# Four more one-element-per-64-KB reads on the ScalarE DMA ring, ahead of the vector c

## The chip, the cores and the metric

The kernel runs on one core of a Trainium2 chip. The metric is the device time of one execution in microseconds (us). Before the change it was 245.06 us, the median of 4 runs.

## The reference

One transformer block on x of 2048 rows by 512 columns, in bf16, with its modulation computed from a vector c:

```python
mod = (silu(c) @ w_mod).reshape(1, 6, 1, 512)       # w_mod 512 x 3072
sa, ca, ga, sb, cb, gb = mod[:, 0], ..., mod[:, 5]
h = layernorm(x) * (1 + ca) + sa
x = x + ga * A(h, wqkv, wo)                          # 32 heads of 16, window of 8 keys, 2 apart
h = layernorm(x) * (1 + cb) + sb
x = x + gb * ((gelu(h @ w_gate) * (h @ w_up)) @ w_down)   # 512 -> 1792 -> 512
```

In A each query attends to the keys at its own row and 2, 4, ... 14 rows before it. The weights are wqkv (512 x 1536), wo (512 x 512), w_gate and w_up (512 x 1792) and w_down (1792 x 512).

## The kernel before, in words

The 2048 rows are cut into five groups of 256, 256, 512, 512 and 512 rows. For each group the kernel normalizes the rows, transposes them, projects to q, k and v, attends, projects back, normalizes again, and runs the gated feed-forward part; the groups overlap. TensorE does the projections and the sums over head dimensions, VectorE the elementwise products of the attention, ScalarE most copies out of PSUM and the activations.

All work is recorded first, as operations with an engine each, and then emitted in one fixed sequence, the list ORDER. Nothing is decided at run time: each engine executes its instructions in that order. The change does not alter the list.

DMAs are issued on two rings: SP's for all loads, stores and transposes, and ScalarE's for four small ones at the very start. In the built program the completion of DMAs is counted on eight semaphores, called lanes here, that are handed out in turn over both rings. A DMA that takes a lane first waits on its issuing engine until the DMA that had the lane before it has landed. So each DMA waits for the one that stands eight places ahead in the program.

The start of the kernel before, by engine:

- ScalarE issues three touches (lines 390 to 398) and then the load of c into `crow` (line 396). A touch reads one pair of bf16 values (4 bytes) from each 64 KB of a tensor into a scratch tile, `touched`, that nothing reads: 48 pairs of w_mod, 24 of wqkv, 32 of x. After that ScalarE loads its activation table and computes scT = silu(c) (line 451).
- SP loads x rows 0 to 255, 256 to 511 and 512 to 1023, then two 512-column blocks of w_mod (line 402), the first two thirds of wqkv (line 384), x rows 1024 to 1535, the last third of wqkv, x rows 1536 to 2047, half of wo, another block of w_mod and the first half of w_gate. The rest of w_gate, w_up and w_down follow between 47 and 72 us.
- TensorE runs 14 warm-up matmuls on zeros (line 435), turns c into columns (`c_ps`, line 448, needs `crow`), runs nine fillers on zeros (line 440), computes the modulation columns `modT_ps` from scT and the two w_mod blocks (line 462), transposes the normalized rows `tp` (line 550) between them, and starts the first projection (`qkv_ps`, line 607).

The first half of w_up is issued at 60.2 us and the second at 62.9 (line 384), into the tile `Wu`; the feed-forward matmuls `g_ps` and `u_ps` (line 800) read `Wg` and `Wu`.

Of the kernel before, what the change touches and what calls it, by code (L numbers as in the profile page):

```python
# [12 lines left out]
BF16 = mybir.dt.bfloat16  # L13
# [52 lines left out]
def _ap(base, free_dims, offset=0):  # L66
    return bass.AP(base.tensor, base.offset + offset, [list(base.ap[0])] + [list(d) for d in free_dims])
# [147 lines left out]
def kernel(  # L215
# [13 lines left out]
    nc = tc.nc  # L229
    P = 128  # L230
# [13 lines left out]
    pl = Plan(tc)  # L244
# [14 lines left out]
    def ctile(shape, dtype, name):  # L259
        t = Tl(None, shape, dtype, name)  # L260
        t.t = const.tile(shape, dtype, name=name)
        return t
# [108 lines left out]
    def load_x(lo, hi, p, after=()):  # L371
        return dma(131e3 * (hi - lo), lambda dq: dq.dma_start(
            out=xs[lo // 4][:, lo % 4:lo % 4 + hi - lo, :],
            in_=A_x[0, lo * P:hi * P, :].rearrange("(c p) d -> p c d", p=P)),
            w=[(xs[lo // 4], c % 4) for c in range(lo, hi)], pri=p, after=after,
            bw=340e3)
# [8 lines left out]
            out=t[:], in_=src[:, lo:hi].rearrange("(t p) n -> p t n", p=P)), w=[t], pri=p, bw=bw, late=late, after=after)  # L385


    touched = ctile([P, 4, 2], BF16, "touched")

    def touch(i, src, n, p):  # L390
        page = 32768
        dma(1.0, lambda dq: dq.dma_start(out=touched[0:n, i, :], in_=bass.AP(src.tensor, src.offset, [[page, n], [1, 2]])),
            w=[(touched, i)], pri=p, ring="act")
# [2 lines left out]
    act(0.5, lambda: nc.scalar.dma_start(out=crow[:], in_=c), w=[crow], pri=-1003, lat=1.7, after=pl.ops[-1:])  # L396
    touch(1, A_wqkv, 24, -1002)
    touch(2, A_x, 32, -1001)
    touches = pl.ops[-2:]
    load_x(0, 2, -1000)  # L400
    for b in (1, 0):
        dma(524e3, lambda dq, b=b: dq.dma_start(
            out=wm01[:, :, b * D:(b + 1) * D], in_=w_mod[:, b * D:(b + 1) * D].rearrange("(t p) n -> p t n", p=P)),
# [7 lines left out]
    for d4 in range(4):  # L411
        dma(131e3, lambda dq, d4=d4: dq.dma_start(
            out=woP[32 * d4:32 * d4 + 32, :, :],
            in_=bass.AP(A_wo.tensor, A_wo.offset + 4 * D * d4, [[16 * D, H], [D, 4], [1, D]])), w=[(woP, d4)],
# [8 lines left out]
    for i in range(2):  # L423
        lo, hi = i * FT // 2, (i + 1) * FT // 2
        dma(918e3, lambda dq, lo=lo, hi=hi: dq.dma_start(
            out=WdP[:, lo:hi, :], in_=B_w_down[lo * P:hi * P, :].rearrange("(t p) n -> p t n", p=P)),
# [422 lines left out]
    for g in range(NG):  # L849
# [11 lines left out]
        if g == PLAIN:  # L861
            for f0 in range(0, FT, 2):
                dve(0.6, lambda f0=f0: nc.vector.tensor_tensor(
                    out=WdP[:, f0:f0 + 2, :], in0=WdP[:, f0:f0 + 2, :], in1=_ap(gbB[:], [[0, 2], [1, D]]),
# [34 lines left out]
```

## Time and profile before

| | |
|---|---|
| time, median of 4 runs | 245.06 us (244.79 to 246.78) |
| the profiled execution | 245.41 us, span 243.7 us |
| TensorE matmul busy | 234.6 us, 96% of the span |
| VectorE, ScalarE, GpSimd busy | 163.4, 148.4, 25.8 us |
| DMA | 29.10 MB, mean 119 GB/s |
| first touch, issue to landing | 2.2 us |
| x touch, issue to landing | 3.1 us |

The profile is of one execution; the span runs from its first to its last instruction. Times in the lines shown below are microseconds from the start of the span; in the lines of instructions in order of time the first number is the start, the second the duration, then engine, source line, operation, and in brackets the idle time before it with what ended it. ACTq and SPq are DMA issues of ScalarE and SP. PEld is TensorE's weight load. A line of the DMA queues gives packets, MB, and the time of the packets as a share of 16 engines over the window.

### The profile page before, as it was taken

How to read it: one execution, taken by the hardware profiler on the slowest of the kernel's cores; microseconds unless marked ns; L12 is line 12 of the kernel's file. 1: busy time of each engine (PE TensorE's matmuls, PEld its weight loads, DVE VectorE, ACT ScalarE, POOL GpSimd, SP SyncE). 2: the span in 40 equal slices, each digit the busy share in tenths (PEclk: the TensorE clock that was granted, in tenths of full speed). 3: DMA queues.
4: the chain of work that ended last, by engine and by line, in shares of the span. 5: the costliest groups of instructions: out<-in, count | busy, mean ns of one | idle time of the engine just before them, and what ended most of it. 6: DMA issues, size and time to landing. Idle time of an engine off the chain costs nothing.

```text
span 243.7 us, 4304 instructions
## 1 busy us (share of the span) xinstructions
PE 234.6 (96%) x1660; PEld 128.0 (53%) x1680; DVE 163.4 (67%) x317; ACT 148.4 (61%) x278; POOL 25.8 (11%) x45
## 2 busy tenths in 40 slices
PE   7799999999999999999999999999999999999993
PEld 3499555544469645675444444444444444444461
DVE  4878998999999999669985577983422413221222
ACT  2188798678958663894588866327467442665400
POOL 1287212002000300120000011000000100000000
PEclk9999999999999999999999999999999999999999
DMA  5998999898999438268021904210000412000011
GB/s 173 351 316 263 191 194 236 186 232 199 260 279 251 141 90 176 65 175 151 7 65 51 219 16 89 43 43 1 3 0 0 106 27 86 0 0 0 3 43 43
DMA packets 38970, 29.10 MB, mean 119 GB/s; under 512 B 14117, under 2 KB 38054, under 8 KB 38950
## 3 DMA queue, kind: packets, MB, share of 16 engines
q1 hardware_dynamic: 38800, 28.83, 49.9%
q8 instruction: 13, 0.21, 0.4%
q14 instruction: 7, 0.06, 0.1%
q10 hardware_dynamic: 150, 0.00, 0.0%
HBM read 21.40 MB, written 4.28 MB: 105 GB/s over the span
## 4 chain that ended last, share of the span: by engine, by line
PE 68%; DVE 16%; DMA 8%; issue 2%; POOL 2%; ACT 2%; SPq 0%; DVEq 0%; ACTq 0%; POOLq 0%
PE y_ps L827 20%; PE u_ps L800 20%; PE g_ps L800 18%; PE x_ps L777 4%; DMA Wu<-in_B_w_up_dram 4%; DMA wqkv<-in_A_wqkv_dram 3%; DVE pq L660 3%; DVE pq L654 3%; DVE pv L752 3%; PE o_ps L762 2%; POOL rstd L522 2%; DVE st L516 2%; DVE xn L526 1%; DMA x_sg<-in_A_x_dram 1%; PE LT L670 1%
## 5 line engine op out<-in xcount | busy, mean ns | idle before, releaser
L800 PE MATMUL u_ps<-h2T,Wu 128*128 128x512 bf16 (+1 forms) x280 | 54.4, 336 | 0.8 <-DMA Wu<-in_B_w_up_dram 0.4
L800 PE MATMUL g_ps<-h2T,Wg 128*128 128x512 bf16 (+1 forms) x280 | 54.7, 337 | 0.1
L827 PE MATMUL y_ps<-WdP,hht 128*128 128x512 bf16 (+1 forms) x230 | 49.1, 366 | 0.4
L809 ACT ACTIVATE gl<-g_ps 128x512 bf16<-128x512 f32 x56 | 33.0, 603 | 25.4 <-PE g_ps L800 25.2
L603 PE MATMUL qkv_ps<-hT,wqkv 128*128 128x512 bf16 (+1 forms) x229 | 43.7, 339 | 0.1
L812 DVE TENSOR_TENSOR hht<-gl,ub 128x512 bf16<-128x512 bf16 x56 | 22.6, 422 | 29.2 <-ACT ub L811 20.9
L811 ACT CAST ub<-u_ps 128x512 bf16<-128x512 f32 x56 | 31.7, 589 | 15.4 <-PE u_ps L800 12.2
L800 PEld LDWEIGHTS <-Wu 128*128 128x128 bf16 x280 | 27.0, 98 | 23.1 <-issue 1.5
L800 PEld LDWEIGHTS <-Wg 128*128 128x128 bf16 x280 | 27.0, 98 | 23.0 <-issue 1.5
L827 PEld LDWEIGHTS <-hht 128*128 128x128 bf16 x238 | 23.1, 98 | 24.6 <-issue 0.4
L522 POOL TENSOR_TENSOR rstd<-rstd,neghalf 128x2 f32<-128x2 f32 x16 | 17.5, 1094 | 162.7 <-DVE rstd L511 140.5
L603 PEld LDWEIGHTS <-wqkv 128*128 128x128 bf16 x232 | 24.9, 114 | 13.6 <-issue 1.3
L654 DVE TENSOR_TENSOR pq<-qT,kT 128x2048 bf16<-128x2048 bf16 x24 | 28.8, 1213 | 0.3
L746 DVE TENSOR_TENSOR pv<-e,vR 128x2048 bf16<-128x2048 bf16 x24 | 28.4, 1216 | 0.0
L538 ACT ACTIVATE h2T<-h2T,modT,scl 128x512 bf16<-128x512 bf16 (+1 forms) x20 | 13.2, 726 | 14.8 <-DMA h2T<-xn 14.8
L840 DVE TENSOR_TENSOR ot<-y_ps,x_sg 128x512 bf16<-128x512 f32 (+1 forms) x13 | 8.2, 647 | 18.5 <-PE y_ps L827 18.5
L781 DVE SCALAR_TENSOR_TENSOR x_sg<-x_ps,x_sg 128x512 bf16<-128x512 f32 x16 | 11.0, 687 | 14.2 <-PE x_ps L777 7.2
L777 PE MATMUL x_ps<-woP,oT 128*128 128x512 bf16 x57 | 14.9, 379 | 0.7 <-DVE rinv L723 0.4
L508 ACT ACTIVATE xn<-x_sg,xsum 128x512 bf16<-128x512 bf16 x16 | 11.5, 721 | 4.3 <-DVE xsum L505 4.3
L516 DVE BATCH_NORM_STATS2 st<-x_sg 128x6 f32<-128x512 bf16 x16 | 10.6, 679 | 3.2 <-DMA x_sg<-in_A_x_dram 3.2
L619 ACT CAST kT<-qkv_ps 128x512 bf16<-128x512 f32 x16 | 9.4, 596 | 1.8 <-PE qkv_ps L603 1.8
L619 ACT CAST qT<-qkv_ps 128x512 bf16<-128x512 f32 x16 | 9.4, 597 | 1.3 <-PE qkv_ps L603 1.3
(93 smaller groups left out, 200.0 us busy)
## 6 DMA issues: line engine op xcount, KB each, us to landing
vR<-scr SPq DMA_DIRECT2D x24, 260.0 KB, 5.3
wm<-in_w_mod_dram SPq DMA_DIRECT2D x6, 512.0 KB, 6.7
vR<-scr SPq DMA_DIRECT2D x8, 264.0 KB, 5.2
out_dram<-ot SPq DMA_DIRECT2D x15, 128.0 KB, 1.8
Wg<-in_B_w_gate_dram SPq DMA_DIRECT2D x2, 896.0 KB, 10.9
Wu<-in_B_w_up_dram SPq DMA_DIRECT2D x2, 896.0 KB, 5.8
WdP<-in_B_w_down_dram SPq DMA_DIRECT2D x2, 896.0 KB, 13.9
scr<-vT SPq DMA_DIRECT2D x6, 264.0 KB, 2.8
```

The costliest lines, as they stand in the source:

```text
L516: dve(0.59, lambda i=i, st=st, c0=c0: nc.vector.bn_stats(out=st[:, i, :], in_=x[g, c0 + i]), r=[x.key(g, c0 + i)], w=[(st, i)], pri=p)
L522: gp(0.65, lambda rstd=rstd: nc.gpsimd.tensor_tensor(out=rstd[:], in0=rstd[:], in1=neghalf[:, 0:2], op=ALU.pow), r=[rstd, neghalf], w=[rst ...
L603: nc.tensor.matmul(ps[:, j - j0, :], lhsT=wqkv[b][:, dt, j:D:4], rhs=h_cols(hT, g, dt), start=(dt == 0), stop=(dt == DT - 1))
L619: act(0.475, lambda t=t, off=off, j0=j0, ps=ps: nc.scalar.copy(out=t[:, j0:j0 + nj, off:off + n], in_=ps[:]), r=[ps], w=[(t, j) for j in r ...
L654: dve(1.14, lambda j=j, wg=wg, t=pq[m]: nc.vector.tensor_tensor(out=t[:], in0=_ap(q[g][:, j, 0:n], [[0, 4], [1, n]]), in1=_ap(k[g][:, j, : ...
L746: dve(1.14, lambda jj=jj, jl=jl, wg=wg, t=pv[m]: nc.vector.tensor_tensor(out=t[:], in0=_ap(e[:, wg, :], [[0, 4], [1, n]]), in1=vR[g][jj][: ...
L777: nc.tensor.matmul(x1_ps[:], lhsT=oT[:, j, c4 * P:(c4 + 1) * P], rhs=woP[:, j, :], start=(j == 0), stop=(j == 3))
L800: nc.tensor.matmul(ps[:, ft - f0, :], lhsT=Wt[ft // 7][:, dt, ft % 7 * P:(ft % 7 + 1) * P], rhs=h_cols(h2, g, dt), start=(dt == 0), stop=( ...
L809: act(0.485, lambda gl=gl, ps=gu[0]: nc.scalar.activation(out=gl[:], in_=ps[:], func=ACT.Gelu_apprx_tanh), r=[gu[0]], w=[gl], pri=p, table ...
L811: act(0.475, lambda ub=ub, ps=gu[1]: nc.scalar.copy(out=ub[:], in_=ps[:]), r=[gu[1]], w=[ub], pri=p)
L812: dve(0.335, lambda gl=gl, ub=ub, ht=ht: nc.vector.tensor_tensor(out=ht[:], in0=gl[:], in1=ub[:], op=ALU.mult), r=[gl, ub], w=[ht], pri=p)
L827: nc.tensor.matmul(y_ps[:], lhsT=hh[ft // nf][:, ft % nf, c4 * P:(c4 + 1) * P], rhs=WdP[:, ft, c0:c0 + w], start=(ft == 0), stop=(ft == FT ...
```

## The change

Four more touches follow the x touch on ScalarE's ring, ahead of `crow`: 8 pairs of wo, 28 each of w_gate, w_up and w_down, into a scratch tile that grows from 4 to 8 columns. They are put into the function of the x touch's operation, so ORDER and the operations in it stay as they are.

```diff
-    touched = ctile([P, 4, 2], BF16, "touched")
+    touched = ctile([P, 8, 2], BF16, "touched")
...
     touch(1, A_wqkv, 24, -1002)
     touch(2, A_x, 32, -1001)
+    first = pl.ops[-1].fn
+
+    def more():
+        first()
+        for i, (src, n) in enumerate(((A_wo, 8), (B_w_gate, 28), (B_w_up, 28), (B_w_down, 28))):
+            nc.scalar.dma_start(out=touched[0:n, 3 + i, :], in_=bass.AP(src.tensor, src.offset, [[32768, n], [1, 2]]))
+
+    pl.ops[-1].fn = more
     touches = pl.ops[-2:]
```

## The prediction

> **What bounds the kernel now.** I read the page first, then the chain of waits over the first 20 us, then the instructions of that stretch in order of time, then the DMA queues in small windows, and last the one later place where a touched tensor is waited for. The page says that TensorE is the bound as a whole:
>
> ```profile
> span 243.7 us, 4304 instructions
> PE 234.6 (96%) x1660; PEld 128.0 (53%) x1680; DVE 163.4 (67%) x317; ACT 148.4 (61%) x278; POOL 25.8 (11%) x45
> ```
>
> So what delays the first real matmul delays the end, unless an idle place later takes it up, and there are only 9.1 us of TensorE idle time in the whole span. The change works on the start. The chain there:
>
> ```profile
> 0.81 2.96 DMA x_sg<-in_A_x_dram
> ...
> 3.79 8.26 DMA wqkv<-in_A_wqkv_dram
> ...
> 12.10 0.84 PE qkv_ps L607 x6
> ```
>
> The first projection waits for the first wqkv third, which lands at 12.05. From 7 us on the DMA engines are full (375, 380, 362, 348, 349 GB/s in the five microseconds from 7 to 12), so the landings of the two w_mod blocks and of wqkv are set by bytes. TensorE is nearly as late, and this is what the chain hides:
>
> ```profile
> 1.26 4.49 PE L435 MATMUL warm_ps<-warm 128*128 128x512 bf16 x14 [1.26 <-DVE neghalf L306]
> 5.71 0.25 PE L448 MATMUL c_ps<-one,crow 1*128 1x1 bf16 x4
> 5.88 2.12 PE L440 MATMUL warm_ps<-warm 128*128 128x512 bf16 x9
> 9.09 0.55 PE L462 MATMUL modT_ps<-scT,wm 128*128 128x1 bf16 x16 [1.08 <-DMA wm<-in_w_mod_dram]
> 9.50 0.61 PE L550 MATMUL tp<-ident,xn 128*128 128x128 bf16 x8
> ...
> 12.10 0.84 PE L607 MATMUL qkv_ps<-hT,wqkv 128*128 128x256 bf16 x6
> ```
>
> The reader is to see an in-order queue: `crow` (the vector c) must be there before `c_ps`, nine filler matmuls stand behind it, and only then come the modulation columns. The one spare is the 1.08 us before 9.09. From 9.09 to 12.10 TensorE has about 0.1 us to spare. The ScalarE queue that brings `crow`:
>
> ```profile
> 0.81 0.44 ACTq L392 DMA_DIRECT2D touched<-in_w_mod_dram  x1
> 1.28 0.64 ACTq L392 DMA_DIRECT2D touched<-in_A_wqkv_dram  x1
> 1.95 0.33 ACTq L392 DMA_DIRECT2D touched<-in_A_x_dram  x1
> 2.31 0.30 ACTq L396 DMA_DIRECT2D crow<-in_c_dram  x1
> ```
>
> It is issued by 2.61, but TensorE gets it at 5.71. Why so late is seen in the DMA queues by window (q1 is SP's ring, q10 ScalarE's). These lines are of 2.93 to 3.80 us, of 3.80 to 4.80 and of 5.20 to 5.31:
>
> ```profile
> q1 hardware_dynamic: 321, 0.31, 100.2%
> q10 hardware_dynamic: 40, 0.00, 2.6%
> ...
> q10 hardware_dynamic: 42, 0.00, 2.2%
> ...
> q10 hardware_dynamic: 1, 0.00, 0.5%
> ```
>
> The 64 packets of the first touch come from 1.88 to 2.68. The second touch's 36 packets start only at 2.93, in threes, and by the packet records each three starts 6 ns after an engine has ended its share of the first x transfer. The third touch's follow in the same way from 3.84, behind the second x transfer. `crow`'s single 1 KB packet comes at 5.21, in the middle of the third x transfer. So each ScalarE DMA waits on each engine for a portion of SP's stream.
>
> **What the Trainium skill says.** "DMA: Bandwidth & Descriptors", section "Queues, rings and completion order", says that a DMA engine takes the rings in turn and drains a whole packet (some 9 to 17 descriptors) of one before it goes to the next. The trace agrees: an x transfer of 256 KB is 16 one-KB pieces per engine, and one such portion lies between two touches. The same page, "Why a DMA increments its semaphore by 16 and not by 1", says that a DMA over few partitions uses the lowest-numbered engines; then engine 0 serves every touch and `crow` as well, so on that engine they stand in one line. No run here shows the engine numbers. "TensorE: Matmul & The Clock Gate", Part 1, puts the clock back to half after an idle window of about 3.4 us; the trace shows the other half of this: 14 warm-up matmuls in 4.49 us are about seven at 0.427 and seven at 0.216, and the nine fillers at 0.235 each are at full speed. On what a first read of a 64 KB stretch costs, no page bears.
>
> **The change, part by part.** Instruction order is unchanged on TensorE, VectorE and GpSimd. On ScalarE four DMAs stand between the x touch and `crow`. Since all DMAs take the eight lane semaphores in turn, four more in front shift who waits for whom. In the built program the touches of w_up and w_down wait for the w_mod touch and for x rows 0 to 255, `crow` waits for x rows 256 to 511; on SP the w_mod blocks wait for the wqkv touch and the x touch (before: nothing and the w_mod touch), the first wqkv third for the wo touch, x rows 1024 on for the w_gate touch, and two more for the w_up and w_down touches. From the third w_mod block on each waits for the same transfer as before.
>
> *ScalarE's issue.* wo and w_gate touches are issued by 3.0 (two of about 0.33). The w_up touch needs 3.0, when the w_mod touch landed (0.81 + 2.2). The w_down touch needs 3.77, when the first x landed. `crow` needs the second x: 3.1 us to landing from an issue at about 1.3, so 4.4. It goes out at 4.45 to 4.75 instead of 2.31. That alone would cost little, for even now it is not served before 5.21.
>
> *The ring.* At 5.21, where `crow` stood, engine 0 serves the wo touch. Then four turns follow: w_gate, w_up, w_down, `crow`, each behind a portion of SP's stream. One 1 KB packet is 16 x 0.87 x 1.002 / 321 = 43 ns, so 16 are 0.7 us; the measured step between touches (2.93 to 3.84) is 0.9. I take 0.8, for part of the portions run at the stalled rates of 4 to 7 us (217 to 282 GB/s): 4 x 0.8 = 3.2 us. `c_ps` starts at 5.71 + 3.2 = 8.9. Bounds: no turn paid, if SP's ring is empty when they come or one turn takes several DMAs, gives `crow` at 4.75 + 0.6 = 5.4, so +0.2; five turns at 0.9 give +4.5.
>
> *TensorE.* `c_ps` and the fillers end 2.3 us after 8.9, at 11.2; the modulation columns start there and not at 9.09: 3.2 - 1.08 = +2.1 us. The rest, 3.0 us of packed work, ends in the first projection at 14.2. scT (0.2 us on ScalarE) lies beside the fillers, and so does the table load of 1.28 us, which starts at about 4.8.
>
> *SP.* The first w_mod block goes at about 4.1 instead of 2.34, the second at about 5.1 (the x touch lands at 1.95 + 3.1), the first wqkv third at about 6. The 1 MB of x occupies the engines until 5.4 to 7.4, so the stream should hardly gap; at worst it loses 1 us, and w_mod and wqkv are then at 10.1, 11.6 and 13.1, still ahead of a TensorE that is at 11.2, 12.7 and 14.2. Cost nothing, covered by the late `crow`; without that cover up to 1 us. The 142 or so extra packets of 9 ns over 14 engines cost 0.1 us each: nothing.
>
> *What the touches may bring.* wo is needed at 46.6 us and has long landed. w_gate's first load runs at 359 GB/s (19.5 to 22 us) untouched, w_down's at 332 to 348 (77 to 81); there is nothing to gain. Only w_up's first load starts slowly, 161 GB/s until 62.6 and then 380, and its second part is waited for:
>
> ```profile
> PEld L800 <- DMA Wu<-in_B_w_up_dram: 0.9, 1, 0.9
> PE u_ps L800 <- DMA Wu<-in_B_w_up_dram: 0.4, 1, 0.4
> ```
>
> The slow stretch holds 1016 packets under 512 B of a transpose, so it is explained without a first read. Gain 0 to 0.4 us, at most 0.9; I take 0.
>
> *Sum.* +2.1 us on the profiled execution, 245.41 to 247.5. That execution stands 0.35 above the median, so the median goes from 245.06 to about 247.1. I take up nothing later: the stretch from 16 to 60 us is data-driven through VectorE (about 95% busy from 25 to 60), so it shifts as a whole.
>
> **The rivals.** *The cover holds* (not slower): `crow` is served in the gaps that SP's later issues leave on its ring, and comes less than 1.1 us later. For it: the new waits do thin SP's stream around 5 us; DMA share in 4 to 5 us is only 0.81 already. Against it: x of 512 rows is still queued then. It decides where `c_ps` starts before 6.8. Time 245.1. With the w_up gain of up to 0.9 on top, *a small gain*: 244.4.
>
> *The clock falls back or the line is longer.* TensorE is idle from 5.75 to 8.9, 3.1 us; at some 0.3 us more a whole idle window is possible and nine fillers take 9 x 0.427 = 3.8 us instead of 2.1: +3.8 and more, 249. Five turns without a fallback give 4.5 - 1.1 = +3.4, 248.5. For it: the stalled rates between 4 and 7 us. Against it: idleness must cover a window whole.
>
> *DMA starved:* the late w_mod issues leave the engines empty for 2 us or more and the wqkv third lands at 14 or later. The size would be that of my forecast, by another path; the chain would then show DMA, not `crow`.
>
> **How the numbers follow.** Forecast (+1.1 to +2.9 us, by `crow` or by starved DMA) 0.47; cover holds 0.27; small gain 0.06; clock or longer line 0.20. A measurement of this kernel can tell about 1%, 2.45 us, from no change. Slower by more than that: 0.20 and a quarter of the forecast's chance, 0.32. Faster by more than that: 0.03, only from causes that I don't see. The rest, 0.65, is within it. Range: 244.4 (the gain's end) to 249.2 (+3.8 and a little).
>
> **What would show it.** `c_ps` at about 8.9 instead of 5.71, the first projection at 14.2 instead of 12.10 with an idle TensorE before `c_ps` of some 3 us, released by `crow`; w_mod waits at 9.09 gone; the nine fillers in about 2.1 us; a first load of w_up with the same slow start at 60 us plus the shift. I am wrong if `c_ps` starts before 6.8, if the shift of the first projection is not found at the end of the span, or if the wait for w_up at 71.3 is gone and the time with it.

## The result, and the profile after

The kernel after takes 245.78 us (median of 42 runs, 244.65 to 247.87), beside 245.06 us for the kernel before, run on the same chip. The ratio is 1.003, with a 95% interval of 1.0017 to 1.0044: a loss of 0.7 us, between 0.4 and 1.1. It is slower, by about a third of the 2.1 us that was forecast. The profiled execution of after took 247.78 us and is one of 6 in 42 (247.35 to 247.87) in which TensorE's mean granted clock was under 0.995 of full, here because the clock was at half from 8.9 to 12.3 us; the others have a median of 245.68, and the first experiment below shows the same kernel at full clock.

The page of after:

```profile
span 246.1 us, 4308 instructions
PE 236.5 (96%) x1660; PEld 128.6 (52%) x1680; DVE 163.4 (66%) x317; ACT 148.3 (60%) x278; POOL 25.6 (10%) x45
```

TensorE's instructions of the start in order of time (start, busy time, what, and in brackets the idle time before it with its releaser):

```profile
1.25 5.27 PE L443 MATMUL warm_ps<-warm 128*128 128x512 bf16 x14 [1.25 <-DVE neghalf L306]
8.49 0.25 PE L456 MATMUL c_ps<-one,crow 1*128 1x1 bf16 x4 [1.97 <-DVE xn L534]
8.68 3.80 PE L448 MATMUL warm_ps<-warm 128*128 128x512 bf16 x9
12.30 0.55 PE L470 MATMUL modT_ps<-scT,wm 128*128 128x1 bf16 x16
...
14.87 0.82 PE L615 MATMUL qkv_ps<-hT,wqkv 128*128 128x256 bf16 x6
```

`c_ps` starts at 8.49 (5.71 before) and the first projection at 14.87 (12.10 before). The bracket at 8.49 names VectorE, but the weight load of `c_ps`, which reads `crow`, waited longer and for the DMA:

```profile
PEld L456 <- DMA crow<-in_c_dram: 2.5, 1, 2.5
```

The nine fillers take 3.80 us here, at half clock, against 2.12 before. The DMA issues on ScalarE in order of time, and then those on SP:

```profile
2.30 0.34 ACTq L404 DMA_DIRECT2D touched<-in_A_wo_dram  x1
...
3.19 0.32 ACTq L404 DMA_DIRECT2D touched<-in_B_w_up_dram  x1
3.89 0.40 ACTq L404 DMA_DIRECT2D touched<-in_B_w_down_dram  x1
4.58 0.23 ACTq L396 DMA_DIRECT2D crow<-in_c_dram  x1
```
```profile
3.94 1.54 SPq L410 DMA_DIRECT2D wm<-in_w_mod_dram  x2
5.65 1.64 SPq L384 DMA_DIRECT2D wqkv<-in_A_wqkv_dram  x2
```

Each issue stands where the prediction had worked it out from the lanes: `crow` at 4.58 (4.45 forecast), w_mod at 3.94 (4.1), wqkv at 5.65 (6). The prediction went wrong in what it derived from them.

### The profile page after: what moved, and what is told of

Read it like the earlier page. It is cut to its first block, busy times and chain, and to the rows that moved or that the text cites. A ratio compares the mean times of both kernels' runs of the same rounds, so it can differ in the third digit from the quotient of the medians.

```text
span 246.1 us, 4308 instructions
## 1 busy us (share of the span) xinstructions
PE 236.5 (96%) x1660; PEld 128.6 (52%) x1680; DVE 163.4 (66%) x317; ACT 148.3 (60%) x278; POOL 25.6 (10%) x45
## 4 chain that ended last, share of the span: by engine, by line
PE 72%; DVE 19%; issue 2%; POOL 2%; ACT 2%; DMA 1%; DVEq 0%; ACTq 0%; POOLq 0%
PE y_ps L835 20%; PE u_ps L808 19%; PE g_ps L808 19%; PE x_ps L785 4%; DVE pq L662 4%; DVE pq L668 3%; DVE st L524 3%; DVE pv L760 3%; PE o_ps L770 2%; POOL rstd L530 2%; PE warm_ps L448 2%; PE LT L678 2%; DVE xn L534 2%; PE qkv_ps L611 1%; DMA x_sg<-in_A_x_dram 1%
## 5 line engine op out<-in xcount | busy, mean ns | idle before, releaser
L546 ACT ACTIVATE h2T<-h2T,modT,scl 128x512 bf16<-128x512 bf16 (+1 forms) x20 | 13.2, 727 | 14.5 <-DMA h2T<-xn 14.5
```

## The experiments

Each was timed beside the kernel before; the ratio is to that, with its 95% interval, and need not be the plain quotient of two medians. `c_ps` and "first projection" are the starts of these matmuls (the first `qkv_ps`) in one profiled execution, 5.71 and 12.10 in the kernel before. "Full clock" below means executions with a mean granted TensorE clock of 0.995 or more.

| kernel | median us | ratio | c_ps | first projection |
|---|---|---|---|---|
| after again | 246.05 | 1.0038 (1.0015 to 1.006) | 7.56 | 12.87 |
| fillers ahead | 245.83 | 1.0027 (1.0009 to 1.0045) | 8.66 | 12.84 |
| three fillers | 245.89 | 1.003 (1.0009 to 1.005) | 7.46 | 14.22 |
| load of c first | 245.91 | 1.0036 (1.0015 to 1.0056) | 7.24 | 12.14 |
| c waits, no reads | 247.2 | 1.005 (1.0023 to 1.0077) | 8.39 | 13.08 |
| two reads | 245.55 | 1.0006 (0.9977 to 1.0035) | 7.29 | 12.93 |
| tiny reads | 245.66 | 1.0033 (1.0017 to 1.0048) | 8.05 | 13.00 |
| reads by GpSimd | 245.5 | 1.0003 (0.998 to 1.0027) | 6.00 | 13.36 |
| no reads at all | 245.27 | 1.0016 (0.9997 to 1.0036) | 5.87 | 12.09 |
| late reads | 245.5 | 1.0014 (0.9992 to 1.0035) | 6.81 | 12.21 |
| pages of w_mod | 246.01 | 1.0029 (1.0007 to 1.0051) | 7.80 | 12.62 |

### After again

No edit.

> The changed kernel once more, for a profile of its usual execution. The one profiled had the nine fillers at half clock (3.80 us for 2.12), and its 247.78 us was among the slowest of its runs. Theory (crow late, fillers behind it): c_ps again at about 8.5, fillers in about 2.1 us where the clock stays at full, first projection at 12.30 - 1.7 + 2.6 = 13.2 us (12.10 before, 14.87 in the profile after), time 245.8. Rival (the DMA stream is what is late): first projection waits for wqkv, and the time does not depend on the fillers' clock.

The loss is there again, and stands at full clock too (median 245.98 of 12, beside 245.09). TensorE's start:

```profile
7.56 0.25 PE L456 MATMUL c_ps<-one,crow 1*128 1x1 bf16 x4 [0.97 <-DMA crow<-in_c_dram]
7.74 2.12 PE L448 MATMUL warm_ps<-warm 128*128 128x512 bf16 x9
9.75 0.55 PE L470 MATMUL modT_ps<-scT,wm 128*128 128x1 bf16 x16
...
11.36 0.55 PE L470 MATMUL modT_ps<-scT,wm 128*128 128x1 bf16 x16
...
12.87 0.84 PE L615 MATMUL qkv_ps<-hT,wqkv 128*128 128x256 bf16 x6
```

`c_ps` starts 1.85 us later than in the kernel before, the first modulation columns 0.66, the projection 0.77. So c came earlier than expected (8.5), and so did the projection (13.2). The chain that ended last (start, duration, what) says what set it:

```profile
2.31 3.73 DMA touched<-in_A_wo_dram
...
6.06 6.77 DMA wqkv<-in_A_wqkv_dram
...
12.87 0.84 PE qkv_ps L615 x6
```

SP issues the first wqkv third when the read of wo, whose lane it takes, has landed at 6.04. The third lands at 12.83 (12.05 before), and the projection starts at once. That is the mark of the rival. The second set of columns waits for the stream as well. Here are the waits of TensorE's weight loads in the first 16 us (total, times, longest), and then the start by stretches of 1 us, where the last three numbers are the granted clock, the DMA share and GB/s:

```profile
PEld L470 <- DMA wm<-in_w_mod_dram: 1.0, 2, 0.6
```
```profile
7.00:8.00 1.00, 0.44 (x6) 0.30 (x7) 1.00 (x5) 0.15 (x1) 0.14 (x2) 1.00 0.66 202
8.00:9.00 1.00, 1.00 (x6) 0.46 (x5) 1.00 (x5) 0.02 (x1) 0.79 (x1) 1.00 0.79 241
9.00:10.00 1.00, 1.00 (x14) 0.45 (x13) 1.00 (x3) 0.00 (x0) 0.00 (x0) 1.00 0.95 303
10.00:11.00 1.00, 1.00 (x23) 0.71 (x19) 0.84 (x3) 0.17 (x1) 0.00 (x0) 1.00 0.97 324
11.00:12.00 1.00, 0.85 (x19) 0.53 (x19) 0.00 (x0) 0.06 (x1) 0.00 (x0) 1.00 1.08 380
```

The kernel before moved 375, 380, 362, 348 and 349 GB/s in these five microseconds, so 1814 KB; here it is 1450 KB, less 364. From 4 to 7 us it was 46 KB more, which leaves 318 KB, or 0.9 us at 350 GB/s. SP's loads were issued later, behind lanes, and the DMA engines ran partly empty at 7 to 9 us. So there are two late paths side by side, c and the stream. Here the stream sets the projection. By c alone it would have started at about 12.3; this is an estimate from the columns at 9.75 and the 2.55 us that the work from there takes where no DMA is waited for ("c waits" below). The next kernels take one path or the other away.

### Fillers ahead

In `emit`, where `ccol` is the operation of `c_ps`:

```diff
+        i = pes.index(self.ccol)
+        pes[i].fill, pes[i + 1].fill = pes[i].fill + pes[i + 1].fill, 0
...
+    pl.ccol = pl.ops[-1]
```

> The kernel after, with the nine filler matmuls put ahead of c_ps, behind the 14 warm-up matmuls, so that nothing but scT stands between the late load of c and the modulation columns, and TensorE is not idle before c_ps. Theory one (the late c with its nine fillers is what delays the first projection): the modulation columns start at about 9.1 and the first projection at about 12.1 to 12.4; median 245.1 to 245.3, as the kernel before. Theory two (in the usual execution the stream of w_mod and wqkv, issued later because of the new lane waits on SP, is as late as c): the columns and the projection wait for DMA, first projection at about 12.7 to 12.9; median 245.7 to 246.0. Both expect the executions with fillers at half clock to be gone, since TensorE no longer idles before c_ps.

TensorE in order of time:

```profile
8.66 0.25 PE L458 MATMUL c_ps<-one,crow 1*128 1x1 bf16 x4
9.16 0.54 PE L473 MATMUL modT_ps<-scT,wm 128*128 128x1 bf16 x16 [0.26 <-ACT scT L462]
...
11.39 0.55 PE L473 MATMUL modT_ps<-scT,wm 128*128 128x1 bf16 x16 [0.79 <-DMA wm<-in_w_mod_dram]
...
12.84 0.84 PE L618 MATMUL qkv_ps<-hT,wqkv 128*128 128x256 bf16 x6
```

Theory two: with c's path shortened, the first columns start at 9.16, nearly as early as before, and the time turns up again one step later as a wait of 0.79 us for w_mod. The projection is 0.74 us late, nearly all of it by the stream, and the loss stays (1.0027). That no execution would fall below full clock was a miss: the mean granted clock was under 0.995 in 6 of 22.

### Three fillers

```diff
+            q.fill = min(q.fill, 3)
```

> The kernel after, with three filler matmuls instead of nine behind c_ps: 6 x 0.235 = 1.4 us less TensorE work behind the late c. Theory one (late c and fillers bind): the modulation columns start 1.1 to 1.4 us earlier than in the kernel after, first projection at about 12.1; median 245.1. Theory two (the stream of w_mod and wqkv binds as well): columns wait for DMA w_mod at about 9.7, first projection at 12.7 to 12.9; median 245.7 to 246.0. If the thinner fillers let the clock fall back to half, modT and the transposes run at twice their time and it is 247 or more under either.

Theory two again by the time, 1.003. The 1.3 us taken out of the fillers became a wait for the stream, as TensorE's order of time shows:

```profile
7.64 0.82 PE L449 MATMUL warm_ps<-warm 128*128 128x512 bf16 x3
9.98 0.59 PE L471 MATMUL modT_ps<-scT,wm 128*128 128x1 bf16 x16 [1.52 <-DMA wm<-in_w_mod_dram]
```

In this execution TensorE fell to half clock at about 9.7, ahead of these columns, which is why its first projection is as late as 14.22. Of all 22 executions 7 had a mean clock under 0.995; the other 15 have a median of 245.52, still 0.5 above the kernel before at full clock (245.00).

### Load of c first

The four reads are issued behind the load of c, not ahead of it:

```diff
+    crow_op = pl.ops[-1]
...
-    first = pl.ops[-1].fn
+    first = crow_op.fn
...
-    pl.ops[-1].fn = more
+    crow_op.fn = more
```

> The same four touches, but issued after the load of c on ScalarE; SP's lane waits stay as in the changed kernel. Theory: c_ps back at about 5.7, so the cost goes, time 245.1 to 245.5 (what is left is SP's stream, whose wqkv third lands some 0.6 us later). Rival (the stream, or the touches themselves, cost the time): 245.8 as in the changed kernel. If touching the later weights brings anything, it shows here: below 244.7.

c is issued at 2.31 and SP's loads wait as in the kernel after. The theory's `c_ps` at 5.7 was missed: it starts at 7.24, behind warm-up matmuls that ended late. The ratio keeps the loss (1.0036), so some loss doesn't need c's late issue. How much is less sure: 7 of the 22 executions were below full clock, and the other 15 have a median of 245.44, 0.35 above that of the kernel before (245.09). The profiled execution doesn't show the loss at the start. Its projection is at 12.14, with the w_mod and wqkv bytes served only 0.2 us later than before (the first 2.62 MB at 10.86 us against 10.62, by the packet records); its first `u_ps` comes 0.24 us later, mostly by a longer wait for w_up (0.57 against 0.37), and that is most of the 0.3 by which its span is longer.

### c waits, no reads

The kernel before, with a ScalarE copy of one x column ahead of the load of c, so that c is issued late and SP's loads are as before:

```diff
+    def load_c():
+        nc.scalar.copy(out=touched[:, 3, 0:1], in_=xs[0][:, 0, 0:1])
+        nc.scalar.dma_start(out=crow[:], in_=c)
...
+    act(0.5, load_c, w=[crow], pri=-1003, lat=1.7, after=pl.ops[-1:])
```

> The kernel before, with no added DMA; ScalarE copies one column of x rows 0 to 127 into scratch before it issues the load of c, so the load waits for the first x transfer (3.8 us) and goes out at about 4.1 instead of 2.31; a second activation-table load comes with the copy. Two theories of why c arrives at 8.49 after the change. Late issue (the load needs about 3 us from its issue whatever stands in the ring): c_ps at about 7.5. Ring turns (as predicted: each touch ahead of it costs a turn of 0.8): nothing stands ahead, so c_ps at 5.7 to 6.3. Time: 245.1 to 245.6 under the first, 245.1 under the second.

ScalarE's issue of the load of c, and TensorE's first use of it, with the columns and the projection that follow:

```profile
3.84 0.26 ACTq L398 DMA_DIRECT2D crow<-in_c_dram  x1
```
```profile
8.39 0.25 PE L452 MATMUL c_ps<-one,crow 1*128 1x1 bf16 x4 [2.25 <-DMA crow<-in_c_dram]
...
10.53 0.54 PE L466 MATMUL modT_ps<-scT,wm 128*128 128x1 bf16 x16
...
13.08 0.82 PE L611 MATMUL qkv_ps<-hT,wqkv 128*128 128x256 bf16 x6
```

A late c alone costs too, if it is late enough: `c_ps` at 8.39 gives a projection at 13.08, and a ratio of 1.005. The stream is whole here (382 and 380 GB/s at 7 to 9 us) and no weight load between the columns and the projection waits for a DMA, so the 2.55 us from 10.53 to 13.08 are the packed length of that stretch. The median of 247.2 lies further off than the ratio: 6 of the 16 executions were below full clock, and the other 10 have a median of 246.22. The profiled one also happens to wait 1.77 us for w_up. This is also the run that breaks the forecast's ring step. No added read stands ahead of `crow`, the ring's last other packet went at 4.44 us, and still `crow`'s packet comes at 7.83, 4.0 us after its issue.

### Two reads

Only w_up and w_down of the four.

```diff
-        for i, (src, n) in enumerate(((A_wo, 8), (B_w_gate, 28), (B_w_up, 28), (B_w_down, 28))):
+        for i, (src, n) in enumerate(((B_w_up, 28), (B_w_down, 28))):
```

> The kernel after with only the reads of w_up and w_down. The load of c then waits for the first w_mod read (landed at about 3.0) and is issued at about 3.1 instead of 4.5; SP's two w_mod blocks still wait for the wqkv and x reads as in the kernel after. Theory one (c's late issue is the larger part): c_ps at about 6.4 to 6.8, fillers done before 9.0, loss 0 to 0.3 us; median 245.0 to 245.4. Theory two (the late stream on SP is enough by itself): c_ps as early, but the modulation columns wait for w_mod at 9.4 to 9.8 and the projection for wqkv, first projection at 12.5 to 12.9; median 245.5 to 245.9.

TensorE in order of time:

```profile
7.29 0.25 PE L456 MATMUL c_ps<-one,crow 1*128 1x1 bf16 x4 [1.39 <-DMA crow<-in_c_dram]
...
11.42 0.55 PE L470 MATMUL modT_ps<-scT,wm 128*128 128x1 bf16 x16 [0.42 <-DMA wm<-in_w_mod_dram]
```

c was issued at 3.21 as expected, but `c_ps` started at 7.29, not at 6.4 to 6.8. The profiled projection (12.93) is theory two's to within 0.03, and so is the median of 245.55; but the interval of the ratio holds 1 and also the loss of the kernel after, so by time this run decides nothing.

### Tiny reads

The same four DMAs, with one pair each:

```diff
-        for i, (src, n) in enumerate(((A_wo, 8), (B_w_gate, 28), (B_w_up, 28), (B_w_down, 28))):
+        for i, (src, n) in enumerate(((A_wo, 1), (B_w_gate, 1), (B_w_up, 1), (B_w_down, 1))):
```

> The kernel after with each of the four added reads cut to one element: the same four DMAs at the same places, so c and SP's loads wait for the same lanes, but 4 packets on the ScalarE ring instead of the 142 added, and 88 stretches of 64 KB fewer are read ahead. Theory one (the lane waits are the loss): c issued at 4.4 to 4.6, SP's w_mod blocks at 3.9 and 5.1 to 5.6, less than 300 GB/s moved in 7 to 9 us, first projection at 12.7 to 12.9; median 245.7 to 246.1. Rival (the packets of the reads, in between SP's, are the loss): SP's stream keeps about 350 GB/s from 7 us on, first projection at 12.1 to 12.4; median 245.0 to 245.4.

ScalarE's issue of the load of c; TensorE in order of time; the stretches of 7 to 9 us:

```profile
4.57 0.23 ACTq L396 DMA_DIRECT2D crow<-in_c_dram  x1
```
```profile
8.05 0.25 PE L456 MATMUL c_ps<-one,crow 1*128 1x1 bf16 x4 [0.77 <-DVE xn L534]
...
13.00 0.84 PE L615 MATMUL qkv_ps<-hT,wqkv 128*128 128x256 bf16 x6
```
```profile
7.00:8.00 1.00, 0.28 (x1) 0.00 (x0) 1.00 (x5) 0.00 (x0) 0.19 (x2) 1.00 0.95 255
8.00:9.00 1.00, 0.95 (x8) 0.57 (x9) 1.00 (x5) 0.17 (x1) 0.79 (x1) 1.00 0.92 270
```

This is the decisive one. ScalarE's ring carried 158 packets, 8 more than before, where the kernel after has 292; and everything is as in the kernel after: c's issue, the 2.9 us from it to its packet (3.3 in after), the thin stream at 7 to 9 us, the wqkv third (it lands at 12.95), and the time, 1.0033 (1.0017 to 1.0048). The first projection, at 13.00, is 0.1 beyond theory one's window. The loss is in the four DMAs' places in the lane order, not in what they read.

### Reads by GpSimd

The four reads with `nc.gpsimd.dma_start`, behind its first masks, so that no lane of the other two rings moves:

```diff
-            nc.scalar.dma_start(out=touched[0:n, 3 + i, :], in_=...)
+            nc.gpsimd.dma_start(out=touched[0:n, 3 + i, :], in_=...)
```

> The same four reads at the same time, but issued by GpSimd in its idle time between 1.6 and 5.8 us, so that the loads on the ScalarE and SP rings wait for exactly the lanes that they wait for in the kernel before. Theory one (the change loses by the lane waits, of c and of SP's loads, not by the reads): c issued at 2.3, w_mod and wqkv as in the kernel before, first projection at 12.1 to 12.2; median 244.9 to 245.3. Rival (the 142 extra packets or the rings' turns cost the stream or c the time): first projection at 12.6 or later, median 245.6 to 246.0. If GpSimd's issuing takes over 1.05 us for each, its rstd at 5.79 is late, and so the first normalised rows: up to 1 us more, with VectorE and not DMA named in front of the transposes.

Issued at 1.5 to 3.8 us, with rstd at 5.82 (5.79 before), so GpSimd lost nothing. The ratio is 1.0003: the reads without the lane waits can't be told from no change. The median of 245.5 lies between the two theories' windows, but the kernel before had 245.2 beside it in this comparison, and only the ratio counts. The profiled execution misses theory one's 12.1, though: the first columns wait for w_mod until 9.77, and then TensorE runs at half clock from about 11.4 to 14.8 us, which makes most of its 13.36. Why w_mod was 0.7 us late there is open.

### No reads at all

The kernel before with its own three reads left out as well.

```diff
+    for o in (pl.ops[-4], pl.ops[-2], pl.ops[-1]):
+        o.fn = lambda: None
```

> The kernel before without its three small reads: the load of c is first on the ScalarE ring, and the first eight loads wait for no lane. Theory one (a first read of a 64 KB stretch costs nothing that can be seen): w_mod and wqkv land as in the kernel before or a few tenths earlier, first projection at 11.8 to 12.1; median 244.8 to 245.2. Rival (the small reads do prepare the large loads): w_mod and wqkv are served at less than 340 GB/s, first projection at 12.6 or later; median 245.6 or more.

Theory one by the profile: the columns at 9.07, the projection at 12.09, and the stream of the kernel before to within a few GB/s, here by stretches of 1 us:

```profile
7.00:8.00 1.00, 1.00 (x6) 0.32 (x4) 0.46 (x1) 0.00 (x0) 0.00 (x0) 1.00 1.06 370
8.00:9.00 1.00, 0.17 (x1) 0.00 (x0) 1.00 (x7) 0.00 (x0) 0.16 (x1) 1.00 1.07 377
```

The median, 245.27, is 0.07 above what theory one gave, and the interval reaches just below 1. Reading one pair per 64 KB ahead of these loads brings nothing that shows.

### Late reads

The four reads issued behind ScalarE's first evictions:

```diff
+                if self.more and o.eng == "act" and o.at > 20.0:
+                    self.more()
+                    self.more = None
```

> The kernel before with the four added reads issued only behind ScalarE's first evictions at about 20 us, so that the first 12 us are those of the kernel before while w_up, w_down and the second half of w_gate are still touched tens of us ahead of their loads. Theory one (the touching brings nothing, and the whole loss of the change comes from the start): first projection at 12.1, the first load of w_up with the same slow start of about 1.5 us at 61 to 62.5; median 244.9 to 245.3. Rival (touching shortens the load of w_up, and the start hid it): no wait for w_up at about 71.3; median 244.3 to 244.8. Should the four reads cost something by themselves (the shifted lanes), it is 245.5 or more.

The start is that of the kernel before (stream 358, 384, 374, 350 and 347 GB/s from 7 to 12 us, projection at 12.21). The median is 0.2 above theory one's range and at the edge of the third case, but the interval, 0.9992 to 1.0035, leaves anything from nothing to the whole loss. A gain of more than 0.2 us from touching w_up is excluded; whether the reads cost something here is not settled. In the profile the first `g_ps` comes 0.47 us later than before (67.72 against 67.25) for 0.11 at the projection, so something after the start took time; what it was wasn't looked into.

### Pages of w_mod

The four reads all read w_mod again, so w_up and the others are not touched:

```diff
-        for i, (src, n) in enumerate(((A_wo, 8), (B_w_gate, 28), (B_w_up, 28), (B_w_down, 28))):
+        for i, (src, n) in enumerate(((w_mod, 8), (w_mod, 28), (w_mod, 28), (w_mod, 28))):
```

> The four added reads keep their sizes, place and waits, but all read w_mod, whose 64 KB stretches the first touch has read already; wo, w_gate, w_up and w_down are not touched. Theory: the stretches read do not matter, 245.8 as in the changed kernel, and the first load of w_up starts as slowly as in both. Rival A (touching the later weights brings a gain that hides part of the cost): slower than the changed kernel by 0.4 us or more. Rival B (reading fresh stretches is what costs): 245.1.

The same loss, 1.0029, with other addresses. In this profile the stream doesn't hold the start up: no weight load waits for w_mod or wqkv, and the projection, at 12.62, follows `c_ps` at 7.80. For w_up, the first `u_ps` matmuls of the kernel after (touched), of "load of c first" (touched), and of "no reads at all" (not touched):

```profile
74.00 1.92 PE L808 MATMUL u_ps<-h2T,Wu 128*128 128x256 bf16 x16
```
```profile
71.94 1.92 PE L809 MATMUL u_ps<-h2T,Wu 128*128 128x256 bf16 x16 [0.57 <-DMA Wu<-in_B_w_up_dram]
```
```profile
71.25 1.92 PE L802 MATMUL u_ps<-h2T,Wu 128*128 128x256 bf16 x16
```

The wait for w_up that the kernel before had (0.37) is found in a touched and is absent in an untouched kernel: it comes and goes by the execution, not by the reads. No kernel here beats the kernel before.

## Why the prediction was wrong, point by point

**What failed: the ring term, 4 x 0.8 = 3.2 us.** The prediction let `crow` stand at 5.21 and charged a turn of 0.8 us for each read ahead of it. The runs show no such turns. By the packet records of after, the four reads' packets went in bursts and were all gone by 6.55; `crow`'s went at 7.90, over a microsecond later, with nothing of its own ring left ahead. With 8 added packets on the ring instead of 142, `crow` came as late after its issue (tiny reads). What goes with the delay is the issue: from 2.31 to 4.58, behind the lane that x rows 256 to 511 hold, and after the issue 2.4 to 4 us as in every kernel whose x is in flight. The prediction had this shift (2.31 to 4.45) and threw it away ("that alone would cost little, for even now it is not served before 5.21"): it read the 2.9 us between issue and packet as a place in a line, where they go along with the issue. At full clock `c_ps` is 1.85 us later, not 3.2. The step between touches was misread too: the third touch's first packets are at 3.62, not 3.84, so the step was 0.7 and not 0.9; and the 0.6 us from issue to packet in the bound "no turn paid" is found in no kernel here, where the least is 0.9.

**What also failed: the "3.0 us of packed work".** From 9.09 to 12.10 the prediction saw "about 0.1 us to spare". But before the change TensorE's weight loads for the columns waited for w_mod twice:

```profile
PEld L462 <- DMA wm<-in_w_mod_dram: 2.1, 2, 1.6
```

The longer wait stands ahead of the first columns, so some 0.5 us of the 2.1 lies inside the stretch. Where no DMA is waited for it takes 2.55 us (c waits) and 2.57 (the profiled execution of after). So `crow` had about 1.5 us of cover, 1.08 and 0.45, and its 1.85 is worth 0.2 to 0.4 us at the projection. By the prediction's own sum it would be 1.85 - 1.08 = 0.77; that the projection did move by 0.77 is chance.

**And the term that was put at nothing: "Cost nothing, covered by the late `crow`".** SP's issues came at 3.94 and 5.65, as worked out, but the stream didn't hold: 318 KB, 0.9 us, were missing at 12 us, and the wqkv third landed at 12.83 instead of 12.05. That is the whole 0.77 of after again, and tiny reads goes the same way (wqkv at 12.95). The size is inside the bound ("at worst it loses 1 us", wqkv at 13.1). The stream wasn't covered because `crow` was over a microsecond less late than forecast and had more slack behind it. Shortening c's path (fillers ahead, three fillers) gave nothing back that the ratios show. Of the four profiles with the lane waits of after, c sets the projection in two (after, at half clock, and pages of w_mod, at 12.62) and the stream in two (after again and tiny reads). So the forecast's sign was right by half of the cause, and its +2.1 was three times the measured 0.7.

**What held.** The instruction order and all issue times; the 1.08 us ahead of the columns; no gain for w_up; the shift travelling undiminished. The first `g_ps` comes 0.78 us later in after again (68.03 against 67.25), for 0.77 at the projection. The 0.4 us by which the span grew less is the wait for w_up, which the profiled execution of the kernel before happened to have.

**The rivals.** "The cover holds" is refuted: `c_ps` was at 7.56 and 8.49, past its limit of 6.8, and the time rose. "DMA starved" had the path of after again and the wrong size: the chain shows DMA and not `crow`, but with 0.9 us of the stream missing instead of 2, and the projection at 12.87 instead of 14. "The clock falls back" describes the profiled execution: fillers of 3.80 us instead of 2.12, after only 1.97 us of idle TensorE and not the 3.1 the prediction counted on. The Trainium skill, "TensorE: Matmul & The Clock Gate", Part 1, asks for an idle window of about 3.4 us, which the idle time here doesn't fill; the measurement decides, and here less was enough. A mean clock under 0.995 also occurs in the kernel before, in 25 of the 190 executions timed beside the experiments, about as often as in the kernel after (6 of 42). In "c waits" (6 of 16), "load of c first" and "three fillers" (7 of 22 each) it is more frequent; why was not tested.

**What stays open.** How much of the loss "load of c first" keeps at full clock, with a profiled start almost that of the kernel before; how often an execution of after goes by c and how often by the stream; and whether the late reads cost anything. One profiled execution each and a resolution of 0.5 us don't settle these.

## What to carry to other kernels

A DMA has a place in the order of lanes besides its bytes: four DMAs put in front shift, by four places, whom each following load waits for, on all rings that share the lanes. Write down those waits first and price the later issue, then the packets. And where a stretch has two paths that end within a microsecond of each other, a "covered" cost is covered only as far as the covering delay is right.

## What the runs showed of the hardware

The 1 KB load of c was served 0.9 us after its issue when it went out first, at 0.80 us (packet at 1.71, no reads at all). In every kernel that issued it at 2.3 us or later, with x in flight, the packet came 2.4 to 4.0 us after the issue: 2.9 before, 3.3 after, 2.9 with 8 added packets on the ring (tiny reads), 4.0 with none left ahead (c waits). The Trainium skill, "DMA: Bandwidth & Descriptors", section "Latency and other measured facts", gives about 0.6 us to the first byte for this kind of ring and an HBM access of 0.2 us on average and 2 us at high load; the 0.9 is near the sum of 0.6 and 0.2, and most of the others lie above 2.6, the sum of 0.6 and 2. These sums are estimates from that page's figures. Which part of the way holds the packet up was not measured.

The 14 warm-up matmuls took between 4.49 us (before) and 6.05 us (load of c first) for the same instructions: the change from half to full clock (some 0.43 and 0.22 us from one to the next) came at a different one each time. A later `c_ps` can therefore be TensorE's own doing: in "load of c first" `crow`'s packet went at 5.76, and `c_ps` at 7.24, straight behind the warm-up.
